# First two token tiles centred instead of normalised for their V products, and the last product of the kernel split over two banks and two store queues

## The chip, the cores and the metric

The kernel runs on one core of a Trainium2 chip. The metric is the device time of one execution in microseconds (us); the profile shows a "span" that is about 1.7 us shorter than that time, because it begins and ends with the recorded instructions. In some rounds the runs of the untouched kernel lay within 0.5 us of each other, in others they spread over as much as 2.3 us, so effects of one microsecond in 720 (0.14%) are at the edge of what can be timed. All runs quoted here are of the fast state; the lowest granted TensorE clock in any of them was 0.997 of full speed.

## The reference, cut to what matters

```python
def _layernorm(x, axis=-1, eps=1e-5):
    m = jnp.mean(x, axis=axis, keepdims=True)
    v = jnp.var(x, axis=axis, keepdims=True)
    return (x - m) / jnp.sqrt(v + eps)

# A_x: 1 x 2048 x 1024, A_wqkv: 1024 x 3072, all bf16
def _A_ref(x, wqkv, wo):                      # linear attention, 32 heads
    q, k, v = ...x @ wqkv...
    phi = lambda t: jnp.where(t > 0, t + 1, jnp.exp(t)) + 1e-6
    pq, pk = phi(q), phi(k)
    kv = jnp.einsum("bhsd,bhse->bhde", pk, v) # sum over all tokens
    z = jnp.einsum("bhsd->bhd", pk)
    # ... num / den, then @ wo

h = x + _A_ref(_layernorm(x), A_wqkv, A_wo)
h2 = h + _B_ref(_layernorm(h), ...)           # gated MLP, 1024 -> 3584 -> 1024
```

The change rests on one identity: a row of `_layernorm(x) @ Wv` is `rstd * ((x - m) @ Wv)`, where `rstd` is one number per token. So the product can start when the mean is known, and the scale can be applied when the result is copied out of PSUM.

## The kernel before: the parts that matter

There are 16 tiles of 128 tokens. For each, VectorE computes statistics and normalises; the normalised tile is transposed, on TensorE (`T1`) for tiles 0 to 3 and by a DMA transpose (`T1d`) for the later ones. Tiles 4 to 15 can then be multiplied in pairs with a Strassen scheme of seven products instead of eight (`sgroup`), which needs sums of weights and sums of x from VectorE. V of tiles 0 to 3 is done directly (`v_piece`), while weights and later tiles are still arriving. Tiles 5 and 6 take their statistics from ScalarE (`ln1_stats_act`: a pass for the mean, and one for the squares).

```python
def fin():                                    # last step of the VectorE statistics
    # bn_aggr (mean, variance), then variance + eps on VectorE, then power -0.5 on POOL
    ...

def v_piece(st, h, mid=None):                 # V of one tile, one half of the columns
    b = alloc_bank(P1_POOL)
    nt = ND2 + h
    for dc in range(NDC):
        if mid is not None and dc == NDC // 2:
            mid()
        mm(bank(b, NW), xnT[:, dc, st * P:(st + 1) * P], wkv[:, dc, nt * NW:(nt + 1) * NW], ...)
    v_copy(b, st, h)                          # ScalarE copies PSUM to SBUF

# sgroup, one Strassen group; X = tiles, W = weights, SX/TW = their sums; [...] cuts
prod(a, X(0, 0), W(0, 0), True, "P1")
ident_act(bank(b), bank(a), ..., name + "fk1")        # ScalarE copies a bank: the "fork"
hook(1)
prod(f, SX(2), TW(2), True, "P7")
# ...
prod(b, SX(1), TW(1), False, "P6")                    # P6 adds onto the fork
# fk2, hook(3), P2 and its phi, hook(4), P5, copy sc, hook(5), P4, hook(6), P3
# phi: ScalarE takes exp, VectorE does min/add and add/max; two of the four phis need
# a VectorE add first (add_phi). What is left over runs inside the NEXT group (pend).

# head
load_x1(0, split=True); load_x1(1); load_wkv(2, half=0, eng="act")
load_x1(2); load_wkv(2, half=1); load_x1(3); load_wkv(3)
pe_dummies(12, P1_POOL + [KVB])               # keep TensorE busy, to end its cold clock
# ... statistics, norm 0, load_wkv(1), T1(0), 3 dummies, norm 1, loads x 4, x 5, load_wkv(0)
v_piece(0, 0, lambda: T1(1))
v_piece(1, 0, lambda: T1(2))
# ... interleaved with weight sums twv/twk, x sums, norms 3 to 5 (see the diff)
k_group(0); v_group(2)                        # K of tiles 0 and 1; V of tiles 4 and 5
```

In the tail, the last product of the MLP accumulates two blocks of 256 columns in one PSUM bank; VectorE adds 512 columns at once and two stores go out on the queue of one engine (SyncE):

```python
for m in range(NM):
    for u in range(2):
        mm(ps[:, bk, u * HNW:(u + 1) * HNW], ...)
# ...
if last and (blk, dh) == (0, 1):
    dma(sl_fin[j], dst, src, "st_%d_%d" % (st, dh), reads=[bsrc])
```

Of the kernel before, what the change touches and what calls it, by code (L numbers as in the profile page):

```python
# [132 lines left out]
def bass_sequential_preLN__linear_attn_block__glu_gated_reglu__prompt_kernel(  # L133
# [71 lines left out]
    with es:  # L205
# [37 lines left out]

        RC = sb("RC", [P, NDC * D], bf16)
        TWk = RC[:].bitcast(f16).rearrange("p (j k c) -> p j k c", j=4, k=KH)
        Ssum = RC[:].bitcast(f16).rearrange("p (s k t) -> p s k t", s=4, k=KH)

# [148 lines left out]
        B_x1 = [bufs("x1_%d_" % i, NBC) for i in range(NX1)]  # L396
        B_xn = bufs("xn_", NXN)
        B_xnT = [bufs("xnT%d_" % s_, 2) for s_ in range(NST)]
        B_wkv = [bufs("wkv%d_" % i, 2) for i in range(NKV)]
# [4 lines left out]
        B_Sx = [bufs("Sx%d_" % i, NST // 2) for i in range(4)]  # L404
        B_at = _Buf("at")
        B_bt = bufs("bt_", 2)
        B_wo = bufs("wo_", ND2)
# [59 lines left out]
        def flat(x):  # L467
            return [b for row in x for b in (flat(row) if isinstance(row, list) else [row])]

        for i in range(2):  # L470
            for b_ in B_pk[NPK + i]:
                b_.over = B_x1[i]
# [299 lines left out]
        def ln_stats_steps(src_full, src_chunk_bufs, name):  # L772
            k = stat_ctr[0] % NSTAT
            stat_ctr[0] += 1

            def bn(c):
                PL.add("dve", lambda e: e.bn_stats(out=st6[:, k, c * 6:(c + 1) * 6],  # L777
                                                   in_=src_full[:, c * BCH:(c + 1) * BCH]),
                       reads=[src_chunk_bufs[c]], writes=[B_st6[k][c]], name=name + "_bn")

            def fin():
                PL.add("dve", lambda e: e.bn_aggr(out=mv[:, k, :], in_=st6[:, k, :]),
                       reads=B_st6[k], writes=[B_mv[k]], name=name + "_aggr")
                PL.add("dve", lambda e: e.tensor_scalar(out=rstd[:, k, :], in0=mv[:, k, 1:2], scalar1=EPS,
                                                        scalar2=None, op0=ALU.add),
                       reads=[B_mv[k]], writes=[B_rstd[k]], name=name + "_ve")
                PL.add("pool", lambda e: e.tensor_tensor(out=rstd[:, k, :], in0=rstd[:, k, :], in1=neghalf[:],
                                                         op=ALU.pow),
                       reads=[B_neghalf], writes=[B_rstd[k]], name=name + "_rstd")
            return k, [lambda: bn(0), lambda: bn(1), fin]  # L790

# [105 lines left out]
        def T1(st):  # L897
# [11 lines left out]
            partial.add(b)  # L909

        def T1d(st):
            k = st % NXN
# [12 lines left out]

        def v_piece(st, h, mid=None):
            b = alloc_bank(P1_POOL)
            nt = ND2 + h
            for dc in range(NDC):
                if mid is not None and dc == NDC // 2:  # L930
                    mid()
                mm(bank(b, NW), xnT[:, dc, st * P:(st + 1) * P], wkv[:, dc, nt * NW:(nt + 1) * NW],
                   dc == 0, dc == NDC - 1, [xnT_buf(st, dc), B_wkv[nt][0 if dc < WKH else 1]], B_bank[b],
                   "v_%d_%d" % (st, h))
            v_copy(b, st, h)

        def v_out(st, j):
# [6 lines left out]
        def v_copy(b, st, j):  # L944
            PL.add("act", lambda e: e.activation(out=v_out(st, j), in_=gw(bank(b)), func=ACTF.Identity),
                   reads=[B_bank[b]], writes=[B_v[st % NV][j]], name="v_%d_%d" % (st, j))

# [673 lines left out]
        def down_pass(ps_, fill):  # L1621
# [20 lines left out]
            def st_out(blk, dh, j, sl, src, bsrc):  # L1642
                st = ps_ * TPP + blk * STB + j
                dst = ov[st * P:(st + 1) * P, dh * NW:(dh + 1) * NW]
                if last and (blk, dh) == (0, 1):
                    dma(sl_fin[j], dst, src, "st_%d_%d" % (st, dh), reads=[bsrc])
                else:
# [27 lines left out]
            def q_add(dst, src, T, H, b, name):  # L1675
                d, bd = quad(dst, T, H)
                x, bx = quad(src, T, H)
                tt(d, qb(b), x, [B_bank[b]] + ([] if src is dst else bx), bd, name)

# [87 lines left out]

            def level2(pi, bks, Q, sg, evac):
                a, f, b, c = bks

                def prod(mi, bk, x, start):
# [5 lines left out]
                    if WSRC[pi][0] == "t" or WLIST[L][2][0] == "s":  # L1777
                        w = w.bitcast(f16)
                    for m in range(NM):
                        for u in range(2):  # L1780
                            mm(ps[:, bk, u * HNW:(u + 1) * HNW], xa[:, m, u * P:(u + 1) * P],
                               w[:, m * HNW:(m + 1) * HNW], start and m == 0 and u == 0, m == NM - 1,
                               xb + [B_wd[ws]], B_bank[bk], "d%d_%d_M%d" % (pi, ps_, mi), skip=True)
                    load_wd_next()
# [12 lines left out]
                def m6():  # L1797
                    prod(6, b, sg(1), False)
                    fork(c, b)

# [4 lines left out]
                def m5():  # L1805
                    prod(5, c, sg(0), False)
                    evac(5, c)

# [4 lines left out]
                def m3():  # L1813
                    prod(3, c, sg(3), False)
                    evac(3, c)

# [12 lines left out]
            level2(5, YB, q_11, sgs[5], ev_out(1, 0, V, O2, sl_out2))  # L1829
            level2(6, XB, q_d4, sgs[6], ev_out(0, 1, U, OS, sl_out))  # L1830

# [57 lines left out]
        load_wkv(2, half=0, eng="act")  # L1889
        act_warm()  # L1890
        load_x1(2)
        load_wkv(2, half=1)
        load_x1(3)
        load_wkv(3)

        pe_dummies(12, P1_POOL + [KVB])
        s0, s1_, s2_, s3 = [ln1_steps(st) for st in range(4)]
        for f_ in s0 + s1_[:1]:
            f_()
        ln1_norm(0)  # L1900
        load_wkv(1)
        T1(0)
        pe_dummies(3, [alloc_bank(P1_POOL)])
        for f_ in s1_[1:] + s2_[:1]:
            f_()
        ln1_norm(1)
        load_x1(4)
        load_x1(5)
        load_wkv(0)
        for f_ in s2_[1:] + s3[:1]:  # L1910
            f_()
        ln1_norm(2)
        for f_ in s3[1:]:
            f_()
# [3 lines left out]

        v_piece(0, 0, lambda: T1(1))
        v_piece(1, 0, lambda: T1(2))  # L1920
        ln1_norm(3)
        x_sums(0)
        v_piece(2, 0)
        m5, q5 = ln1_stats_act(5)
        m5()
        twv.pop(0)()
        v_piece(0, 1, lambda: T1(3))
        twk.pop(0)()
        ln1_stats(4)
        q5()  # L1930
        v_piece(1, 1)
        twk.pop(0)()
        ln1_norm(4)
        T1d(4)
        m6, q6 = ln1_stats_act(6)
        v_piece(3, 0)
        m6()
        ln1_norm(5)
        T1d(5)
        twk.pop(0)()  # L1940
        v_piece(2, 1)
        q6()
        twv.pop(0)()
        twk.pop(0)()
        twv.pop(0)()
# [54 lines left out]
        for p in range(NP_):  # L2000
            nq = NQ.get(p, (0, 0))
            hooks, sq = kv_hooks(p, nq)
            if p == NP_ - 1:
                hooks[7] = lambda: kvaccs(NP_ - 2)
# [236 lines left out]
```

## Time and profile before

The time before was 722.88 us (722.54 to 722.95, three runs). The page of the profiled run says where it goes. The first fence is from that page: span, busy table, busy tenths by fortieth of the span, and the chain that ended last.

```profile
span 721.0 us, 12872 instructions
PE 714.9 (99%) x4905; PEld 380.3 (53%) x4905; DVE 588.1 (82%) x1024; ACT 358.2 (50%) x623; POOL 110.7 (15%) x177
PE   8999999999999999999999999999999999999998
...
PE ps L763 94%; DMA RE<-RE 1%; DMA RAB<-RXH 1%; DVE RWG L981 0%; DMA RE<-in_A_x_dram 0%; ACT RXH L801 0%; PE ps L902 0%; DVE RX L1065 0%; DVE RE L1639 0%; DVE st L777 0%; DVE RXH L1230 0%; DVE RE L1126 0%; ACT RXH L1256 0%; DVE RW L956 0%; DVE RX L846 0%
```

TensorE (PE) is the bound, at 99% busy. Only its first and last fortieth show an 8. So only two places look worth anything: the microseconds before TensorE starts, and the tail. The Trainium skill ("TensorE: Matmul & The Clock Gate", Part 1: The HAM clock gate) says that a 512-column matmul starts every 426.7 ns while TensorE is cold and every 215.7 ns when warm. The trace agrees: 0.427 us for the dummies, 0.216 us later.

The timeline of TensorE in the first 34 us: start, duration of the group, engine, line, what it does, and in brackets how long TensorE sat idle before it and what ended the wait.

```profile
6.46 0.61 PE L902 MATMUL ps<-ident,RXH 128*128 128x128 bf16 x8 [0.50 <-DVE RXH L831]
...
7.85 1.02 PE L763 MATMUL ps<-RAB 128*128 128x512 bf16 x4
...
24.02 2.03 PE L763 MATMUL ps<-RC,RWG 128*128 128x512 f16 x8
25.89 1.03 PE L763 MATMUL ps<-RAB 128*128 128x512 bf16 x4
...
30.20 2.06 PE L763 MATMUL ps<-RW,RWG 128*128 128x512 f16 x8
```

The first V matmul starts at 7.85 us.

The timeline of VectorE (DVE), same kernel: the path to the first normalised tile, and then the last weight sums, the first phi of the K group (L846) and the first add of the K group (L1065).

```profile
4.93 0.15 DVE L784 TENSOR_SCALAR rstd<-mv 128x1 f32<-128x1 f32 x1
...
5.77 0.55 DVE L831 TENSOR_SCALAR RXH<-RE,mv,rstd 128x1024 bf16<-128x1024 bf16 x1
...
25.58 1.22 DVE L956 TENSOR_TENSOR RW<-RAB,RW 128x2048 f16<-128x2048 bf16 x1
27.58 0.29 DVE L846 TENSOR_SCALAR RX<-RX 128x512 bf16<-128x512 bf16 x1 [0.78 <-ACT RX L842]
...
28.84 0.68 DVE L1065 TENSOR_TENSOR RX<-ps,RX 128x512 f32<-128x512 f32 x1
```

Between 4.93 and 5.77 us the first tile waits for the variance and its power; this is what the change goes around.

The tail before, from the timeline of all engines:

```profile
714.83 2.67 PE L763 MATMUL ps<-RE,RAB 128*128 128x256 f16 x23
...
716.80 2.27 SPq L561 DMA_DIRECT2D out_dram<-RX  x4
717.54 0.69 DVE L1639 TENSOR_TENSOR RX<-ps,RE 128x512 bf16<-128x512 f32 x1 [0.77 <-PE ps L763]
```

The last matmul starts at 717.234; the last add takes 0.69 us; the last two stores are issued at 718.26 and 718.64 and land at 719.95 and 720.44.

### The profile page before, as it was taken

Reading aid. Unit: us, or ns where it says so; the run is one execution under the profiler, and the core shown is the slowest. Engines: PE = TensorE matmul, PEld = TensorE weight load, DVE = VectorE, ACT = ScalarE, POOL = GpSimd, SP = SyncE. Lnnn points to the kernel's source line nnn. Section 1 sums busy time; section 2 is a strip of 40 time slices with the busy share of each in tenths; the row PEclk is TensorE's granted clock in tenths of the full one; section 3 lists DMA queues with packets and bytes.
Section 4 is the critical chain, followed back from the end, with each engine's and each line's share of the span. In section 5 each row is a group of like instructions: output and inputs, shape, how many; then the busy total and the mean of one; then the engine's idle time right before and its main releaser. Section 6 shows DMA issues by size and latency. Waiting matters only on the chain.

```text
span 721.0 us, 12872 instructions
## 1 busy us (share of the span) xinstructions
PE 714.9 (99%) x4905; PEld 380.3 (53%) x4905; DVE 588.1 (82%) x1024; ACT 358.2 (50%) x623; POOL 110.7 (15%) x177
## 2 busy tenths in 40 slices
PE   8999999999999999999999999999999999999998
PEld 3444444444444444444444558865554555548887
DVE  7888867899776889888988787887889877887984
ACT  4877667764832466677756111144454545423010
POOL 2411100000450103331321001310000000000331
PEclk9999999999999999999999999999999999999999
DMA  9663244024998797999999999993464572037996
GB/s 313 212 106 72 46 132 160 3 30 76 217 229 257 223 287 232 275 303 316 301 271 271 305 257 324 314 216 114 140 179 128 161 256 72 1 103 252 323 316 177
DMA packets 192989, 143.64 MB, mean 199 GB/s; under 512 B 51872, under 2 KB 170400, under 8 KB 192928
## 3 DMA queue, kind: packets, MB, share of 16 engines
q1 hardware_dynamic: 188224, 138.50, 65.7%
q0 software_dynamic: 4032, 3.67, 3.5%
q8 instruction: 38, 0.62, 0.4%
q10 hardware_dynamic: 672, 0.66, 0.3%
q14 instruction: 23, 0.19, 0.1%
HBM read 98.76 MB, written 32.51 MB: 182 GB/s over the span
## 4 chain that ended last, share of the span: by engine, by line
PE 94%; DVE 2%; DMA 2%; issue 1%; ACT 1%; POOL 0%; SPq 0%; DVEq 0%; ACTq 0%
PE ps L763 94%; DMA RE<-RE 1%; DMA RAB<-RXH 1%; DVE RWG L981 0%; DMA RE<-in_A_x_dram 0%; ACT RXH L801 0%; PE ps L902 0%; DVE RX L1065 0%; DVE RE L1639 0%; DVE st L777 0%; DVE RXH L1230 0%; DVE RE L1126 0%; ACT RXH L1256 0%; DVE RW L956 0%; DVE RX L846 0%
## 5 line engine op out<-in xcount | busy, mean ns | idle before, releaser
L768 ACT ACTIVATE ps<-ps 128x512 f32<-128x512 f32 (+1 forms) x192 | 108.9, 567 | 221.5 <-PE ps L763 214.7
L763 PE MATMUL ps<-RC,RO 128*128 128x512 f16 x616 | 143.0, 369 | 0.0
L763 PE MATMUL ps<-RH,RWG 128*128 128x512 bf16 x448 | 108.1, 379 | 0.0
L763 PEld LDWEIGHTS ps<-RC,RO 128*128 128x128 f16 x616 | 60.3, 98 | 63.5
L763 PE MATMUL ps<-RC,RWG 128*128 128x512 f16 x320 | 76.8, 379 | 0.0
L763 PEld LDWEIGHTS ps<-RH,RWG 128*128 128x128 bf16 x448 | 43.8, 98 | 46.9
L1448 DVE TENSOR_TENSOR RAB<-ps,RAB 128x512 bf16<-128x512 f32 x56 | 37.3, 686 | 30.4 <-PE ps L763 30.4
L763 PE MATMUL ps<-RH,RO 128*128 128x512 bf16 (+1 forms) x256 | 61.2, 379 | 0.0
L1648 POOL DMA_DIRECT2D out_dram<-RX x20 | 17.9, 1256 | 263.3 <-DVE RX L1639 221.0
L763 PE MATMUL ps<-RW,RE 128*128 128x512 bf16 x256 | 57.6, 379 | 0.2 <-DMA RE<-RE 0.2
L763 PE MATMUL ps<-RAB 128*128 128x512 bf16 (+2 forms) x270 | 57.1, 351 | 0.1
L763 PE MATMUL ps<-RW,RAB 128*128 128x256 f16 (+3 forms) x362 | 52.9, 301 | 0.0
L763 PEld LDWEIGHTS ps<-RC,RWG 128*128 128x128 bf16 (+1 forms) x320 | 30.0, 98 | 39.8 <-ACT ps L768 5.8
L768 ACT ACTIVATE RE<-ps 128x512 f32<-128x512 f32 (+1 forms) x64 | 31.5, 503 | 37.8 <-PE ps L763 37.8
L763 PEld LDWEIGHTS ps<-RW,RAB 128*128 128x128 f16 (+1 forms) x362 | 35.3, 98 | 14.5
L1639 DVE TENSOR_TENSOR RE<-ps,RE 128x512 f32<-128x512 f32 x44 | 30.2, 687 | 14.3 <-PE ps L763 13.8
L768 ACT ACTIVATE RAB<-ps 128x512 bf16<-128x512 f32 x56 | 33.3, 594 | 16.9 <-PE ps L763 16.5
L1332 DVE TENSOR_TENSOR RO<-RWG 128x1024 f16<-128x1024 bf16 x54 | 36.9, 684 | 4.8 <-DMA RWG<-in_B_W_up_dram 4.8
L763 PEld LDWEIGHTS ps<-RH,RO 128*128 128x128 f16 (+1 forms) x256 | 24.4, 98 | 29.9 <-ACT RX L768 1.5
L1443 ACT ACTIVATE RAB<-RAB 128x1024 bf16<-128x1024 bf16 x28 | 29.5, 1055 | 19.2 <-DVE RAB L1434 18.6
L1434 DVE TENSOR_TENSOR RAB<-ps,RE 128x512 bf16<-128x512 f32 x56 | 37.2, 685 | 2.2 <-PE ps L763 1.9
L763 PEld LDWEIGHTS ps<-RAB 128*128 128x128 bf16 (+1 forms) x270 | 26.0, 98 | 24.4 <-ACT RAB L905 1.1
(163 smaller groups left out, 1159.1 us busy)
## 6 DMA issues: line engine op xcount, KB each, us to landing
RWG<-in_B_W_gate_dram SPq DMA_DIRECT2D x28, 512.0 KB, 6.2
RWG<-in_B_W_up_dram SPq DMA_DIRECT2D x28, 512.0 KB, 5.2
RW<-l_scr SPq DMA_DIRECT2D x20, 448.0 KB, 5.9
RW<-in_B_W_down_dram SPq DMA_DIRECT2D x14, 512.0 KB, 5.3
t_scr<-RW SPq DMA_DIRECT2D x14, 512.0 KB, 4.8
l_scr<-RX SPq DMA_DIRECT2D x7, 1024.0 KB, 6.0
RE<-l_scr SPq DMA_DIRECT2D x15, 448.0 KB, 5.6
RE<-in_A_x_dram SPq DMA_DIRECT2D x23, 256.0 KB, 3.7
```

What stands on the lines that cost most here:

```text
L763: lambda e: e.matmul(out_ap, lhsT, rhs, start=start, stop=stop, skip_group_check=skip),
L768: PL.add("act", lambda e: e.activation(out=dst, in_=src, func=func), reads=reads, writes=writes, name=name)
L1332: PL.add(eng, lambda e: e.tensor_tensor(out=tb(j, u), in0=f0(u), in1=f1(u), op=ALU.subtract), reads=[B_w[i + x] for x in r] + ([B_T[k + x] ...
L1434: PL.add("dve", lambda e: e.tensor_tensor(out=d, in0=src, in1=ftmp[:, u, :], op=ALU.add), reads=[bsrc, B_s5[u]], writes=[db], name=name)
L1443: PL.add("act", lambda e: e.activation(out=d, in_=d, func=ACTF.Relu), reads=[], writes=db, name=name)
L1448: PL.add("dve", lambda e: e.tensor_tensor(out=d, in0=bank(b), in1=d, op=ALU.mult), reads=[B_bank[b]], writes=[db], name=name)
L1639: PL.add(eng, lambda e: e.tensor_tensor(out=dst, in0=in0, in1=in1, op=op), reads=reads, writes=writes, name=name)
L1648: PL.add("pool", lambda e: e.dma_start(dst, src, accum_op=ALU.add), reads=[bsrc], writes=[B_hscr[st]], slot=sl, name="acc_%d_%d" % (st, dh))
```

## The change

The intent is twofold. In the head, tiles 0 and 1 are centred in halves as soon as their mean is known, transposed on TensorE, and multiplied; the copy of their V products from PSUM applies `rstd`. Their normalised versions are still needed for K and Q, so they are made too, and are now transposed by two DMA transposes. In the tail, the two halves of the last product go to two PSUM banks, one half first; VectorE adds the first half while TensorE computes the second, and the stores alternate between the queues of SyncE and ScalarE.

The core of the diff (cuts marked with `...`):

```diff
+        def centre(st, hf):
+            PL.add("dve", lambda e: e.tensor_scalar(out=xn[:, 2 + st, c], in0=x1[:, st, c], scalar1=mv[:, k, 0:1],
+                                                    scalar2=None, op0=ALU.subtract), ...)
+        def T1c(st, hf):
+            ... # four 128x128 transposes of the centred half on TensorE, one ScalarE copy to xcT
         def v_copy(b, st, j):
-            PL.add("act", lambda e: e.activation(out=v_out(st, j), in_=gw(bank(b)), func=ACTF.Identity),
+            sc, rd = (1.0, []) if st >= 2 else (rstd[:, v_k[st], :], [B_rstd[v_k[st]]])
+            PL.add("act", lambda e: e.activation(out=v_out(st, j), in_=gw(bank(b)), func=ACTF.Identity, scale=sc),
...
         act_warm()
-        load_x1(2)
         load_wkv(2, half=1)
-        load_x1(3)
+        load_x1(2)
         load_wkv(3)
+        load_x1(3)
-        pe_dummies(12, P1_POOL + [KVB])
+        pe_dummies(9, [KVB] + P1_POOL)
...
+        for hf in range(2):
+            centre(0, hf)
+            T1c(0, hf)
+        pe_dummies(2, [alloc_bank(P1_POOL)])
... # the same for tile 1; load_wkv(1) in between
         ln1_norm(0)
-        T1(0)
+        T1d(0)                                # DMA transpose, then load of x tile 4
...
         ln1_norm(1)
-        load_x1(4)
-        load_x1(5)
+        T1d(1)                                # DMA transpose, then load of x tile 5
         load_wkv(0)
...
-        v_piece(0, 0, lambda: T1(1))
-        v_piece(1, 0, lambda: T1(2))
+        v_piece(0, 0, {5: lambda: T1c(1, 0), 7: lambda: T1c(1, 1)})
+        ln1_norm(2)
+        v_piece(1, 0)
... # V pieces, weight sums, x sums and statistics in a new order
-        m6, q6 = ln1_stats_act(6)
+        m6, q6a, q6b = ln1_stats_act(6, True) # squares of tile 6 in two halves, inside the K group
         v_piece(3, 0)
         m6()                                  # mean of tile 6: still in front of the K group
...
+            if p == 0:
+                hooks[1], hooks[3] = q6a, q6b
```

```diff
 # tail
-                    dma(sl_fin[j], dst, src, "st_%d_%d" % (st, dh), reads=[bsrc])
+                    dma(sl_fin[j], dst, src, "st_%d_%d" % (st, dh), reads=[bsrc], eng=("sp", "act")[j % 2])
...
-                    for m in range(NM):
-                        for u in range(2):
-                            mm(ps[:, bk, u * HNW:(u + 1) * HNW], ...)
+                    two = isinstance(bk, tuple)
+                    for m, u in [(m, u) for u in range(2) for m in range(NM)] if two else \
+                            [(m, u) for m in range(NM) for u in range(2)]:
+                        bu = bk[u] if two else bk
+                        mm(ps[:, bu, u * HNW:(u + 1) * HNW], ...)
```

## The prediction

> **What bounds the kernel.** TensorE. The page gives PE 99% busy of a 721.0 us span; the busy table by stage shows PE full in nearly every stretch after 60 us, and the wait list for PE between 26 and 700 us has only 0.5 us. A warm 512-column matmul starts every 0.216 us, a 128-column transpose every 0.056 us. So only two places are worth anything: the time before TensorE runs gaplessly, and the tail after its last matmul.
>
> **Head, before (timeline).** Tile 0 lands at 3.34-3.51 us; statistics 3.36-4.89; variance add 4.93; power on POOL 5.17-5.74; normalise 5.77-6.32; transposes 6.46; ScalarE copy 7.11; first V matmul 7.85. TensorE then runs to the first K product at about 23.15 us with one 0.14 us gap.
>
> **Head, after.** Centring needs only the mean; half a tile is about 0.3 us (0.55 us for 1024 columns). So transposes start near 5.35, the copy of the first half near 5.8, the first V matmul near 6.5: 1.35 us earlier, with as many transposes and matmuls as before. The nine cold dummies (0.427 us each) still cover the cold clock, which ended at 5.16 us. Scaling on the four V copies reads a per-partition operand; the Trainium skill ("ScalarE: Activation LUTs", What ACT_TABLE_LOAD costs) puts about 93 ns on each; no run has shown it here, and it is off the path.
>
> **What takes some back.**
> - Loads are serial: 256 KB per 0.68 us, 512 KB per 1.5 us by their landings. The second half of the first V weights should land near 7.4 us (needed 7.4), x tile 2 near 8.1 instead of 6.64, so the third tile's normalise ends near 11.6: TensorE waits about 0.3 us.
> - VectorE, second busiest up to 52 us, gets four centrings (+1.2 us).
> - Two DMA transposes (about 1.1 us of all DMA engines each) now sit among the loads. The first K weights land near 20 us (17.7 before; needed 22.2), x tile 6 near 22 us. Its mean on ScalarE stands in front of the copy that opens product 6 of the first K group: TensorE may wait about 0.6 us there.
> - VectorE's chain to the first KV accumulation (34.9 us, where TensorE already waited 0.33 us) comes only about 0.6-0.9 us earlier.
>
> Net head gain: 0.8 us (0.2 to 1.3).
>
> **Tail.** Before: last matmul ends near 717.5; one 128x512 add of 0.69 us to 718.23; stores issued at 718.26 and 718.64 on one queue, landed 719.95 and 720.44. After: the first half is summed under the second half's seven matmuls (7 x 0.109 us), 128x256 takes about 0.42 us, the last store is issued at once on the other queue: about 0.7 us saved. Two banks are needed because two engines must not touch one bank at once (Trainium skill, "PSUM — Partial Sum Buffer", PSUM bank collisions). Two 128x256 forks for one of 128x512 cost ScalarE 0.15 us, hidden.
>
> **Sum.** 722.88 - 0.8 - 0.7, rounded: 721.3 us, a gain of 0.2%. 80% range 720.1 to 722.6. Faster by over 2%: 0.01; within 2%: 0.98; slower by over 2%: 0.01.
>
> **What would show it.** First V matmul near 6.5 us; first K product near 22.2 (23.15 before); first KV accumulation 0.6-0.9 us earlier than 34.9; from there a constant lead to the last matmul; last store landing 2.3 us after the last matmul instead of 2.9.
>
> **What would make it wrong.** DMA transposes that hold up the loads by several us (the first K group waits for weights, the head gain vanishes); or the ScalarE mean and VectorE backlog costing nothing (then near 720.7).

## More of the kernel before

The eight matmuls at 24.02 are P7 and P6 of the first K group, the eight at 30.20 are P7 and P6 of the next group (V of tiles 4 and 5). In both, P6 follows P7 almost without a break (0.13 and 0.16 us from the start times of the single matmuls).

Note the 0.78 us: VectorE's list of sums ends at 26.80, and it then waits for ScalarE. That is all the slack VectorE has at this point.

ScalarE (ACT), same kernel: the mean of x tile 6 and, behind it in ScalarE's order, the fork that P6 of the K group needs.

```profile
21.31 1.06 ACT L801 ACTIVATE RXH<-RE 128x1024 bf16<-128x1024 bf16 x1 [0.42 <-DMA RE<-in_A_x_dram]
...
24.36 0.60 ACT L768 ACTIVATE ps<-ps 128x512 f32<-128x512 f32 x1
```

## The result, and the profile after

The changed kernel took 723.08 us (median of four runs, 722.52 to 723.54) against 722.85 us for the kernel before in the same rounds (722.54 to 722.95, four runs). The ratio is 1.0004, with a 95% interval of 0.9986 to 1.0021. Ratios here are the mean time of one kernel's fast runs over that of the other's of the same rounds, so they are not quite the ratio of the medians quoted. The predicted gain of 1.6 us, a ratio of 0.9978, lies outside that interval: it did not come. The time of 723.08 lies outside the predicted range of 720.1 to 722.6.

The lines of the page that answer to those of before, now for the kernel after:

```profile
span 721.8 us, 12822 instructions
PE 710.7 (98%) x4846; PEld 380.0 (53%) x4901; DVE 589.0 (82%) x1030; ACT 358.9 (50%) x626; POOL 111.4 (15%) x178
...
PE ps L769 93%; DMA RE<-in_A_x_dram 2%; SPq L567 1%; ACT RXH L809 0%; DVE RWG L1016 0%; DVE RE L857 0%; DVE RX L1100 0%; ACT ps L774 0%; DVE RE L1674 0%; DVE RX L854 0%; DVE st L783 0%; DVE RW L991 0%; SPq L571 0%; ACT RX L850 0%; DVE RWG L1614 0%
```

The span is 0.8 us longer. The chain has a new second entry: 2% of the span, some 14 us, now runs through loads of x (`in_A_x_dram`), and the queue of SyncE (`SPq`) with its DMA transpose (L571) is on it. Before, the loads of x were at 0%.

TensorE, kernel after, the same stretch as before:

```profile
6.67 1.02 PE L769 MATMUL ps<-RAB,RC 128*128 128x512 bf16 x4
7.90 0.39 PE L769 MATMUL ps<-RAB,RC 128*128 128x512 bf16 x1 [0.21 <-DMA RAB<-in_A_wqkv_dram]
...
23.23 1.03 PE L769 MATMUL ps<-RC,RWG 128*128 128x512 f16 x4
25.67 1.04 PE L769 MATMUL ps<-RC,RWG 128*128 128x512 f16 x4 [1.42 <-ACT ps L774]
...
30.86 1.03 PE L769 MATMUL ps<-RW,RWG 128*128 128x512 f16 x4
32.12 1.04 PE L769 MATMUL ps<-RW,RWG 128*128 128x512 f16 x4 [0.23 <-ACT ps L774]
```

The first V matmul is 1.18 us earlier, as intended, and P7 of the first K group is still 0.79 us ahead of before. Then P6 of the K group waits for the fork on ScalarE. Counted from one matmul start to the next, less the usual 0.216 us, that wait is 1.58 us, and 0.39 us at P6 of the following group, where before had 0.13 and 0.16. So the lead of 0.79 us becomes a lag of 0.90 us (-0.79 + 1.45 + 0.24).

ScalarE, kernel after, says what the fork was waiting behind:

```profile
23.50 1.06 ACT L809 ACTIVATE RXH<-RE 128x1024 bf16<-128x1024 bf16 x1 [1.12 <-DMA RE<-in_A_x_dram]
...
25.03 0.59 ACT L774 ACTIVATE ps<-ps 128x512 f32<-128x512 f32 x1
```

The mean of x tile 6 started at 23.50 (before: 21.31), when the tile had landed. The fork stood behind it.

VectorE, kernel after: the new centrings, the last weight sum, the first phi and the first add.

```profile
5.01 0.62 DVE L922 TENSOR_SCALAR RXH<-RE,mv 128x512 bf16<-128x512 bf16 x2
...
26.70 1.23 DVE L991 TENSOR_TENSOR RW<-RAB,RW 128x2048 f16<-128x2048 bf16 x1
28.47 0.29 DVE L854 TENSOR_SCALAR RX<-RX 128x512 bf16<-128x512 bf16 x1 [0.55 <-ACT RX L850]
...
29.74 0.68 DVE L1100 TENSOR_TENSOR RX<-ps,RX 128x512 f32<-128x512 f32 x1
```

The last weight sum ended 1.13 us later than before (27.93 against 26.80), and the first phi and the first add came 0.9 us later. The first matmul that accumulates KV followed at 35.80 instead of 34.91.

The tail after:

```profile
715.80 3.22 PE L769 MATMUL ps<-RE,RAB 128*128 128x256 f16 x28
...
718.32 0.81 SPq L567 DMA_DIRECT2D out_dram<-RX  x2
718.33 1.54 ACTq L567 DMA_DIRECT2D out_dram<-RX  x2
719.06 0.42 DVE L1674 TENSOR_TENSOR RX<-ps,RE 128x256 bf16<-128x256 f32 x1 [0.34 <-PE ps L769]
```

The last matmul starts at 718.751 and the last store, issued at 719.52, lands at 721.215: 2.46 us from one to the other, against 3.21 us before (720.44 - 717.234). The tail gave 0.75 us. Its parts can be read off: the last add is 0.27 us shorter (0.42 instead of 0.69), the last store is issued 0.04 us after that add instead of 0.41 (it no longer follows another store on the same queue), and it lands 1.70 us after its issue instead of 1.80. No run had only one of the two edits, the two banks or the two queues.

The landing times, read from the semaphore records of the DMA engines, are these. "first" and "last" are the first and the last of the 16 DMA engines; the transfer is complete at the last.

| load | before, issued | first / last | after, issued | first / last |
|---|---|---|---|---|
| first V weights, half 0 | 1.23 | 5.61 / 5.82 | 1.24 | 5.87 / 6.36 |
| first V weights, half 1 | 2.18 | 7.78 / 8.12 | 1.72 | 7.36 / 7.86 |
| DMA transpose of tile 0 | none | | 8.32 | 16.01 / 16.17 |
| x tile 4 | 7.09 | 15.16 / 15.49 | 12.55 | 16.74 / 16.79 |
| DMA transpose of tile 1 | none | | 13.09 | 17.51 / 17.70 |
| x tile 5 | 9.20 | 15.84 / 16.18 | 15.18 | 18.29 / 18.99 |
| second half of the first K weights | 10.10 | 18.85 / 19.19 | 16.27 | 21.12 / 22.77 |
| x tile 6 | 11.41 | 19.51 / 21.23 | 16.89 | 21.81 / 23.41 |

Two things show. Everything behind the transposes is 1.3 to 3.6 us late at its last landing. And the last landing of x tile 6 trails the first by 1.6 to 1.7 us in both kernels. The Trainium skill ("DMA: Bandwidth & Descriptors", Why a DMA increments its semaphore by 16 and not by 1) says that the engines of one transfer finish independently and only the full count means that all data is there; the trace agrees. In both traces one engine had a packet of instruction fetch (16 KB; 1.10 us from 18.96 before, 0.93 us from 19.34 after) among its work shortly before; whether that made it the late one, the trace does not say.

### The profile page after: what moved, and what is told of

The parts are those of the page before. It is cut to its first block, busy times and chain, and to the rows that moved or that the text cites. A ratio compares the mean times of both kernels' runs of the same rounds, so it can differ in the third digit from the quotient of the medians.

```text
span 721.8 us, 12822 instructions
## 1 busy us (share of the span) xinstructions
PE 710.7 (98%) x4846; PEld 380.0 (53%) x4901; DVE 589.0 (82%) x1030; ACT 358.9 (50%) x626; POOL 111.4 (15%) x178
## 4 chain that ended last, share of the span: by engine, by line
PE 93%; DMA 2%; DVE 2%; issue 1%; ACT 1%; SPq 1%; ACTq 0%
PE ps L769 93%; DMA RE<-in_A_x_dram 2%; SPq L567 1%; ACT RXH L809 0%; DVE RWG L1016 0%; DVE RE L857 0%; DVE RX L1100 0%; ACT ps L774 0%; DVE RE L1674 0%; DVE RX L854 0%; DVE st L783 0%; DVE RW L991 0%; SPq L571 0%; ACT RX L850 0%; DVE RWG L1614 0%
## 5 line engine op out<-in xcount | busy, mean ns | idle before, releaser
L769 PE MATMUL ps<-RH,RO 128*128 128x512 bf16 (+1 forms) x228 | 55.2, 379 | 1.5
L769 PE MATMUL ps<-RAB 128*128 128x512 bf16 (+2 forms) x237 | 49.7, 348 | 0.1
L769 PEld LDWEIGHTS ps<-RW,RE 128*128 128x128 bf16 x256 | 24.0, 98 | 28.7 <-DVE dtmp L1236 0.6
```

What stands on the lines that cost most here:

```text
L769: lambda e: e.matmul(out_ap, lhsT, rhs, start=start, stop=stop, skip_group_check=skip),
```

## The experiments

Fifteen kernels ran, one of them twice (`e4` and `e4b`). Each edit is given against the kernel before or after. The texts in quotes use letters for theories; the sense is the one that the text gives. The theories are these:

- **Late load.** The two DMA transposes delay x tile 6; its mean on ScalarE holds the fork; TensorE waits at P6 of the K group.
- **VectorE's list.** The four centrings (two took 0.62 us, so 1.2 us in all) and their later waits lengthen VectorE's list; whatever lead TensorE has, it waits for VectorE (directly or through ScalarE) at the next group.
- **Both, one behind the other.** Taking the first away only uncovers the second.
- **Rivals.** The order of ScalarE's own work; the DMA transposes as such, by their place in the queue; the tail not paying.

All results (us; "before" is the kernel before of the same rounds):

| run | base and edit | median (range), runs | before | ratio (95%) |
|---|---|---|---|---|
| e1_tail | before + tail | 722.11 (721.83-722.44), 5 | 722.79 | 0.9987 (0.9975-0.9999) |
| e2_head | before + head | 724.14 (723.62-725.05), 5 | 722.79 | 1.0017 (1.0005-1.0030) |
| e3_x6_first | after, x tile 6 loaded before K weights | 723.06 (722.97-726.53), 6 | 722.79 | 1.0010 (0.9994-1.0025) |
| e4_mean_later | after, mean of tile 6 behind the fork | 723.24 (722.04-724.28), 5 | 722.79 | 1.0001 (0.9989-1.0013) |
| e4b_mean_later | the same again | 722.26 (722.05-722.58), 4 | 722.69 | 0.9994 (0.9981-1.0008) |
| e6_pe_transposes | after, TensorE instead of DMA transposes | 724.22 (723.72-724.85), 5 | 722.53 | 1.0022 (1.0010-1.0034) |
| e7_transposes_last | after, the transposes last in the queue | 723.14 (722.71-723.72), 5 | 722.53 | 1.0007 (0.9994-1.0019) |
| e8_last_and_mean | e7 and e4 | 723.36 (723.04-723.79), 5 | 722.53 | 1.0010 (0.9998-1.0022) |
| e9_before_two_transposes | before + two idle DMA transposes | 725.51 (724.13-727.75), 6 | 722.53 | 1.0042 (1.0028-1.0057) |
| e10_norm_on_act | after, norms 0 and 1 on ScalarE | 723.16 (722.57-723.27), 5 | 722.69 | 1.0004 (0.9991-1.0018) |
| e11_norm_act_mean | e10 and e4 | 722.34 (722.09-722.67), 5 | 722.69 | 0.9995 (0.9983-1.0008) |
| e12_before_centrings | before + four idle centrings | 723.79 (722.99-724.57), 5 | 722.69 | 1.0014 (1.0001-1.0026) |
| e13_mean_and_pool | e4, one weight sum on POOL | 722.87 (722.79-723.52), 5 | 723.60 | 0.9993 (0.9980-1.0005) |
| e14_norm_mean_pool | e11, one weight sum on POOL | 722.41 (722.07-722.69), 5 | 723.60 | 0.9985 (0.9971-0.9998) |
| e15_one_sum_less | e4, one weight sum left out (wrong result) | 721.87 (721.40-724.04), 5 | 722.47 | 0.9988 (0.9975-1.0002) |
| e16_squares_later | e4, squares of tile 6 later too | 722.03 (721.99-722.74), 5 | 722.47 | 0.9992 (0.9980-1.0005) |

No ratio is clear of 1 by more than half a per cent, and many intervals hold 1. So most of the argument below rests on the profiled runs, where one can follow the lead or lag of TensorE against the kernel before from mark to mark. "Lead" means the start of the same instruction on TensorE, compared with the profiled run of before. A profiled run is a single execution.

### Head and tail apart

`e1_tail` is the kernel before with only the tail part of the diff; `e2_head` is the kernel before with only the head part.

```diff
 # e1_tail: of the change, only these
+                if isinstance(b, tuple): ...            # two adds of 256 columns
+            c2 = (c, spare) if spare is not None else c
+    level2(6, XB, q_d4, sgs[6], ev_out(0, 1, U, OS, sl_out), YB[3] if last else None)
+    ... eng=("sp", "act")[j % 2]
 # e2_head: everything else
```

> The kernel before with only the tail of the change (last product's halves in two banks, its stores on two queues). Theory A (the tail gained about 0.75 us, as the profile of after shows: 2.46 us from the last matmul's start to the last landing instead of 3.21, and the head gave it back): 0.6 to 0.8 us under before. Rival T (the tail gained nothing in the timed runs): same as before within 0.2 us.

> The kernel before with only the head of the change (centred tiles, scale on the copy, new order of loads). Theory A: the head loses what the tail gains: 0.5 to 1.3 us over before, with the 1.6 us wait of TensorE before product 6 of the first K group. Rival T (head and tail both near zero): within 0.2 us of before.

The tail alone is 0.9987 and the head alone 1.0017; the product is 1.0004, which is the ratio of the whole change. In us, the tail gives 0.9 and the head costs 1.2 (by the medians 0.7 and 1.35), where 0.7 and a gain of 0.8 were predicted; both intervals only just exclude 1. In the trace of `e1_tail` TensorE runs as before up to its last matmul (it starts at 717.154, before 717.234), and the span is 720.2 instead of 721.0. In that of `e2_head` the wait at P6 of the K group is there again, at 1.85 us, TensorE lags by 0.97 us at 32 us, and by 0.84 us at the end. So the tail did what it should, and the fault lies in the head.

### Is it the late load of x tile 6?

`e3_x6_first` puts the load of x tile 6 ahead of the first K weights, and `e4_mean_later` takes the mean of tile 6 from in front of the fork.

```diff
 # e3_x6_first, against after
-        load_wkv(0)
...
         ln1_norm(2)
+        load_wkv(0)
 # e4_mean_later and e4b_mean_later, against after
         v_piece(3, 0)
-        m6()
...
-                hooks[1], hooks[3] = q6a, q6b
+                k4_ = hooks[4]
+                hooks[1], hooks[3], hooks[4] = m6, q6a, lambda: (q6b(), k4_())
```

> After with the load of x tile 6 put before the two loads of the first K weights. Theory A (the mean of tile 6 on ScalarE waits for tile 6, and the copy that opens product 6 stands behind it): tile 6 lands near 20 instead of 23.4 us, TensorE's wait there falls from 1.58 to about 0.6 us (the mean itself, 1.25 us, still stands before the copy), total about 0.9 us under after. Rival B (VectorE's backlog after four more centrings is the limit): the total stays within 0.3 us of after, the wait moves to the second V group or the first KV accumulation.

> After with the mean of tile 6 moved on ScalarE behind the copy that opens product 6 of the first K group, its squares two products later; loads as in after. Theory A: that wait of 1.58 us is gone, perhaps 0.2 us at product 5; total 1.1 to 1.5 us under after. Rival B (VectorE): as for the run before, at most 0.3 us.

> The kernel with the mean of tile 6 moved, again, because the profile of its first run fell on an execution in which one DMA engine brought the first weights 2.3 us late. Theory AB: where the first weights land near 6.2 us, no wait before product 6 of the first K group, but product 6 of the second V group still starts no earlier than 31.8 us, because VectorE's first K result comes near 28 us. Theory A2 alone: product 6 of the second V group starts near 30.6 us.

The profiled runs of `e3` and of the first `e4` were spoilt by something else: one of the 16 DMA engines delivered the first V weights late (last landing 8.49 and 8.18 us instead of 6.36), so TensorE stood still for 1.8 and 2.1 us between 6 and 9 us. In `e4` it then ran its matmuls at 0.427 us until 11.7 us, that is, with the cold clock. For that reason `e4` was run again as `e4b`. Its profiled run was clean: the lead of 1.07 us at P7 is still 1.07 behind P6. The wait of 1.58 us at P6 is down to 0.16. So the late load is a cause of that wait, and the order of ScalarE's work is how it reached TensorE. But the lead did not last. TensorE, VectorE and ScalarE of `e4b`:

```profile
31.35 1.04 PE L769 MATMUL ps<-RW,RWG 128*128 128x512 f16 x4 [0.58 <-ACT ps L774]
```

```profile
20.99 1.23 DVE L991 TENSOR_TENSOR RC<-RAB 128x2048 f16<-128x2048 bf16 x1 [0.76 <-DMA RAB<-in_A_wqkv_dram]
...
27.71 0.29 DVE L854 TENSOR_SCALAR RX<-RX 128x512 bf16<-128x512 bf16 x1
```

```profile
29.69 0.63 ACT L850 ACTIVATE RX<-RX 128x512 bf16<-128x512 f32 x1 [0.70 <-DVE RX L1100]
```

VectorE's first phi starts at 27.71 with no wait just before it: VectorE has become the limit. (Before, it came at 27.58 after a wait of 0.78.) But earlier in its list, at 20.99, VectorE had waited 0.76 us for K weights, which stand behind the transposes; so its lateness here is not all work of its own. ScalarE idles 0.70 us for VectorE's add (L1100), and the fork of the next group stands behind that exp. P6 of the next group waits 0.74 us, P3 of the K group had waited 0.47, and the lead of 1.07 us is a lag of 0.13 at 32 us and of 0.02 at the end. The span, 720.3 us, is that of the tail alone (720.2). `e3`'s timed runs do not differ from after's (five of its six are between 722.97 and 724.01), and its profile says nothing clean. `e4b` fell between its two forecasts: P6 of the next group started at 31.35, earlier than the 31.8 of theory AB and later than the 30.6 of A2.

### Is it the DMA transposes?

`e6` makes the transposes of tiles 0 and 1 on TensorE again; `e7` puts the two DMA transposes behind all the early loads; `e8` is `e7` with the mean moved. `e9` goes the other way: it adds two DMA transposes, into a space that nobody reads, to the kernel before.

```diff
 # e6_pe_transposes, against after
-        T1d(0)
+        load_x1(4)
-        T1d(1)
+        load_x1(5)
-        v_piece(1, 1)
-        v_piece(2, 0)
+        v_piece(1, 1, {4: lambda: T1(0)})
+        v_piece(2, 0, {4: lambda: T1(1)})
 # e7_transposes_last, against after: loads as in e6, then
         ln1_norm(2)
+        for st in range(2):
+            dma_t(sl_tx[st], xnT[:, :, st * P:(st + 1) * P], xn[:, st, :], "T1d_late", ...)
... # x_sums(0) moves behind two of the K weight sums; scratch of tile 5's mean moves
 # e8_last_and_mean: e7, and m6 moved as in e4
 # e9_before_two_transposes, against before
-        load_x1(4)
-        load_x1(5)
+        for st in range(2):
+            dma_t(sl_tx[st], xcT[:, st], xn[:, st, :], "extra", ...)
+            load_x1(4 + st)
```

> After with the two early DMA transposes done on TensorE instead (16 transposes of 0.056 us, 0.9 us of TensorE). Theory A2 (the two transposes sit in the one queue of loads and make every load behind them about 2.2 us later, and TensorE, 0.8 us ahead, now meets those loads; which wait ends last, weights or tile 6, changes with the order): x tile 6 lands again near 21.2 us, K weights near 17.7 and 19.2, the 1.6 us wait before product 6 of the first K group falls under 0.3 us; total 0.3 to 0.7 us under after. Rival B (four centrings on VectorE): total 0.9 us over after (the price of the transposes).

> After with the two DMA transposes behind the K weights and x tile 6 in the queue, and VectorE's sums of tiles 0 and 1 behind the two K weight sums that need only weights. Theory A2: wait before product 6 falls from 1.6 to about 0.6 us, total about 0.9 us under after. Rival B: within 0.3 us of after.

> The same and the mean of tile 6 moved behind the copy that opens product 6. Theory A2: no wait over 0.3 us in the first K group, total 1.2 to 1.5 us under after, the fastest so far. Rival B: within 0.3 us of after.

> The kernel before with two DMA transposes more, into a place nothing reads, at the same place among the loads where the change has them; nothing else. Theory A2: loads behind them 2.2 us later, x tile 6 near 23.4 us, TensorE waits 1.0 to 1.6 us in the first K group, total 0.9 to 1.5 us over before. Rival B: no change.

`e9` is the clearest. Two transposes that compute nothing cost the kernel before 3 us (1.0042). TensorE's timeline shows where:

```profile
21.21 6.22 PE L766 MATMUL ps<-RAB 128*128 128x512 bf16 x27 [3.09 <-ACT RAB L908]
```

x tile 5 landed at 19.45 instead of 16.18, ScalarE's mean of tile 5 waited for it, and the copy of transposed tile 3 stood behind that mean. The lag is 3.1 us at 32 us and 2.8 us at the end. SyncE's issue of the first transpose occupied its queue for 5.07 us here and 4.11 us in the kernel after, that of the second for 2.07 and 2.04 us, and later loads on that queue were issued only afterwards. This is not the price of a transpose alone. From 22 to 40 us the same traces have transposes of the same shape whose issue took 1.2 to 1.3 us (one in `e9` took 2.06), and in the kernel before two plain loads at 4.9 and 7.1 us took 2.06 and 2.01 us to issue, where most took 0.4 to 0.5. The long issues fall where many loads are outstanding; that this backlog makes them long was not tested. The 3 us are also twice what was expected of `e9` (0.9 to 1.5), since the late load met another place of ScalarE's order than the one named. That the transposes delay the loads is therefore shown, and that such a delay reaches TensorE through ScalarE's order too.

But removing the delay is not enough. In `e6` x tile 6 landed at 19.92 and P6 of the K group waited only 0.36 us. With the 16 transposes back on TensorE (16 times 0.056 us) its lead at P7 was only 0.05 us, and VectorE's first add came 0.42 us late, so that the lag at 32 us was 0.41 us. Two further waits of 1.2 and 1.3 us, at 167 and 239 us, made it 2.7 us at the end; the trace puts both to VectorE, but nothing here says why it was late. In `e7` and `e8` the lag just behind P6 of the K group was nothing (-0.08 and -0.02 us), but VectorE now waited for the late transposes (in `e7` 1.32 us before norm 4 and 0.31 us before x sum 0), and its first phi came at 29.16 and 29.22 us. P6 of the next group then waited 1.36 and 1.29 us, for a lag of 1.6 us in both. Both were forecast to gain 0.9 to 1.5 us over after if only the loads mattered; neither did. Wherever the transposes go, the time is lost at the next place.

### Is it VectorE's list?

`e12` adds the four centrings, and nothing else, to the kernel before, just in front of x sum 0. `e10` and `e11` take work off VectorE: the norms of tiles 0 and 1 are made on ScalarE from the centred copies (with `e11` also moving the mean).

```diff
 # e12_before_centrings, against before
         ln1_norm(3)
+        for i in range(4):
+            PL.add("dve", lambda e, i=i: e.tensor_scalar(..., scalar1=mv[:, 2, 0:1],
+                                                         scalar2=None, op0=ALU.subtract), ...)
         x_sums(0)
 # e10_norm_on_act, against after
-        ln1_norm(0)
-        T1d(0)
-        ln1_norm(1)
-        T1d(1)
-        load_wkv(0)
+        def norm_act(st): ...      # activation, Identity, scale=rstd, from xn[2 + st] to xn[st]
+        v_piece(0, 0, {5: ..., 7: lambda: (T1c(1, 1), norm_act(0), norm_act(1))})
+        T1d(0)
+        T1d(1)
+        load_wkv(0)
 # e11_norm_act_mean: e10, and m6 moved as in e4
```

> The kernel before with four centrings more (about 1.2 us of VectorE) into a place nothing reads, before the first sums of tiles 0 and 1; loads and TensorE as before. Theory AB: VectorE has little idle time up to 52 us, so TensorE waits 0.5 to 1.0 us more in the second V group or the first KV accumulation; total 0.4 to 1.0 us over before. Theory A2 alone: same as before within 0.2 us.

> After with the full normalisation of tiles 0 and 1 (two operations of 0.55 us on VectorE, needed only for the DMA transposes) done on ScalarE from the centred copies; loads in the same order. Theory A2 alone (only loads are late): same as after within 0.3 us. Theory AB (the loads and VectorE's backlog hold TensorE at about the same time, so that removing one leaves the other): VectorE's chain up to the first K result about 0.5 to 1 us earlier where it does not wait, but the 1.6 us wait before product 6 stays: total 0 to 0.4 us under after.

> The same and the mean of tile 6 moved behind the copy that opens product 6 (both suspected waits relieved). Theory AB: first K result on VectorE near 27.5 us (28.47 in after), product 6 of the second V group starts near 31.2 us (32.12 in after), total 0.7 to 1.2 us under after, near 722.0. Theory A2 alone: as the mean moved alone (0 to 0.3 us under after).

`e12` costs 1.0014, or 1.0 us, with an interval that just excludes 1. In its profiled run the first phi came at 28.01 instead of 27.58, and now without a wait. VectorE (the four centrings and the phi) and TensorE (P6 of the next group) of `e12`:

```profile
13.21 1.14 DVE L1925 TENSOR_SCALAR RC<-RXH,mv 128x512 bf16<-128x512 bf16 x4
...
28.01 0.28 DVE L848 TENSOR_SCALAR RX<-RX 128x512 bf16<-128x512 bf16 x1
```

```profile
31.64 1.04 PE L765 MATMUL ps<-RW,RWG 128*128 128x512 f16 x4 [0.17 <-ACT ps L770]
```

So the added work used up the slack of 0.78 us, and the phi came 0.43 us late; the lag of TensorE at 32 us was 0.42 us, and 0.31 at the end. Not all of this is the centrings: they hold VectorE for 1.05 us (13.21 to 14.26), and this execution was already 0.24 us late in front of them (norm 3 at 12.75 instead of 12.51) and 0.10 us late at P7 of the K group. About 0.3 us of TensorE's lag (0.42 less 0.10) is theirs. The timed 1.0 us is more, but its interval begins at 0.1 us, and one of the five times (724.57) is 3.2 us over its span instead of the usual 1.7. By the spans the medians differ by 0.5 us (721.4 against 720.9).

`e10` and `e11` freed about 1.0 us on VectorE, but VectorE then waited 0.94 and 1.09 us for the first K weights, which had landed at 21.5 and 21.3 us. The weights stand behind the DMA transposes, so the freed time could not be used. In `e11`, then, VectorE was late through a wait for weights more than through work. `e10` waited 1.94 us at P6 of the K group; `e11`, with the mean moved, led by 0.74 there, lagged by 0.45 at 32 us and by 0.06 at the end. Timed, `e11` was 0.7 us under after, at the low edge of what theory AB expected.

### Can VectorE be relieved so that it counts?

`e13` and `e14` move one V weight sum from VectorE to POOL, in four pieces. `e15` leaves the sum out altogether and puts zeros in its place. Its result is wrong (relative error 0.83), but its timing is that of a kernel whose VectorE has one 1.2 us sum less. `e16` tests the rival that it is the order of ScalarE's work: the two halves of the squares of tile 6 move later.

```diff
 # e13_mean_and_pool: e4, and
+        twv.pop(1)
+        def twv_pool(kk):
+            PL.add("pool", lambda e: e.tensor_tensor(out=tw_v(0)[:, kk, :], ..., op=ALU.subtract), ...)
... # four calls behind v_piece(1, 0)
 # e14_norm_mean_pool: e11, and the same
 # e15_one_sum_less: e4, and
+        PL.add("pool", lambda e: e.memset(TWv[:, 0], 0.0), writes=[B_TWv[0]], name="twv0")
+        twv.pop(1)
 # e16_squares_later: e4, but
+                hooks[1] = m6
+                hooks[4], hooks[5] = lambda: (q6a(), k4_()), lambda: (q6b(), k5_())
```

> The kernel with the mean of tile 6 moved, and one of VectorE's weight sums (1.22 us, the first of the V sums) given to POOL in four pieces. Theory AB (VectorE's backlog takes back the 1.07 us of lead that TensorE had at product 6 of the first K group): VectorE's first K result about 0.5 us earlier (27.2 instead of 27.71), the wait of 0.74 us before product 6 of the second V group halves, total 0.3 to 0.7 us under the mean moved alone, near 721.7. Rival C (ScalarE, with the moved mean in the first K group, takes it back): VectorE finishes earlier and then waits for ScalarE, TensorE as before, total within 0.2 us of the mean moved alone (722.3).

> The same with the full normalisation of tiles 0 and 1 on ScalarE too. Theory AB: VectorE waits for the K weights near 21 us instead, so little on top: within 0.3 us of the run before. Rival C: ScalarE has more to do, 0 to 0.4 us slower than the run before.

> The kernel with the mean of tile 6 moved, and one of VectorE's weight sums (1.22 us) left out altogether: POOL fills its place with zeros before VectorE starts, so the result is wrong on purpose and POOL takes no time beside VectorE. Theory AB (VectorE's backlog): the wait of 0.74 us before product 6 of the second V group falls under 0.4 us and TensorE keeps more of its lead; total 0.3 to 0.8 us under the mean moved alone (722.26), near 721.7. Rival C (ScalarE's order): VectorE finishes 1.2 us earlier and waits for ScalarE; total within 0.2 us of 722.26.

> The kernel with the mean of tile 6 moved, and its two squares on ScalarE one and two products later still, with nothing taken off VectorE. Rival C: the 0.47 us wait before product 3 of the first K group goes, total 0.3 to 0.5 us under 722.26. Theory AB: that wait goes too, but the time turns up before product 6 of the second V group, where VectorE is as late as before; total within 0.2 us of 722.26.

POOL was no relief. VectorE of `e13`, the K weight sum that ran beside POOL's pieces:

```profile
17.56 2.17 DVE L991 TENSOR_TENSOR RC<-RAB 128x2048 f16<-128x2048 bf16 x1
```

The same sum takes 1.22 us elsewhere, and a norm beside POOL took 1.29 us instead of 0.55. The Trainium skill ("SBUF — State Buffer", Who interferes with whom) says that a VectorE instruction with two SBUF inputs contends with a GpSimd (POOL) instruction that reads SBUF, that a `tensor_scalar` such as the norm can contend too, in a two-port mode, and that the one of the two that issues later is held up. The trace agrees that they hold each other up: what VectorE lost on three instructions (0.95, 0.74 and 0.75 us) is more than the 1.2 us it was spared. `e14`'s ratio of 0.9985 leans on a high set of runs of before (median 723.60); its own median of 722.41 is no better than `e4b`'s 722.26. So `e13` missed the gain that theory AB forecast, and because of POOL the two runs say little about that theory.

`e16` took away the wait before P3 of the K group, and its lead there was 0.79 us. Then P6 of the next group waited longer, 1.07 instead of 0.74 us. TensorE and VectorE of `e16`:

```profile
31.34 1.04 PE L769 MATMUL ps<-RW,RWG 128*128 128x512 f16 x4 [0.90 <-ACT ps L774]
```

```profile
28.96 0.68 DVE L1100 TENSOR_TENSOR RX<-ps,RX 128x512 f32<-128x512 f32 x1
```

VectorE's first add, which before was at 28.84, is at 28.96: 0.12 us late. TensorE's lag behind P6 is 0.12 us. `e4b` had 28.97 and a lag of 0.13. The two kernels reach P6 with different leads, and leave it together, at the time VectorE sets. This speaks against the order of ScalarE's work in the K group as the cause of what is left. Timed, `e16` was 0.23 us under `e4b`, between the two forecasts, so the trace has to decide.

The traces of all runs can be asked the same question. In sixteen of the eighteen profiled runs, before and after among them, P6 of that group starts 2.37 to 2.38 us after VectorE's first add (before: 31.22 and 28.84; after: 32.12 and 29.74), however early TensorE was. The other two are `e4` and `e15`, where the first weights were so late that TensorE did not wait there (2.45 us). So VectorE's add sets this place, in the kernel before too. Why the add is late differs. In after, VectorE still waited 0.55 us for ScalarE in front of the first phi, so there the late fork set it: without that wait the phi would have come about 0.26 us after that of before (an estimate, from 26.70 and the 1.14 us between the same two starts in `e4b`), and not 0.9. In `e4b`, `e7`, `e8` and `e11` VectorE had waited for transfers, and in `e16` 0.45 us for the statistics of tile 5, which came at 23.7 us instead of 21.7. Only `e12` has the centrings alone. How the lateness of `e4b` and `e16` divides between the centrings and these waits was not separated.

`e15` was meant as the counter-proof. Its profiled run had the late DMA engine again (8.09 us), so its offset to before is of no use, but the waits are. VectorE and TensorE of `e15`:

```profile
29.79 0.29 DVE L855 TENSOR_SCALAR RX<-RX 128x512 bf16<-128x512 bf16 x1 [1.46 <-ACT RX L851]
```

```profile
32.65 1.89 PE L770 MATMUL ps<-RW,RWG 128*128 128x512 f16 x8
```

With one sum less, VectorE has 1.46 us of slack at the first phi, and P7 and P6 of the next group run through as eight matmuls without a break. Its four other runs took 721.40 to 722.58 us, and the lowest three are below every run of `e4b` and `e16`. The median is 0.4 us below `e4b`'s; this fits, but is too small to be called a measured gain. The late run also shifts VectorE and TensorE against each other, since the loads were not as late as TensorE was, so this profile alone is not a clean proof; that VectorE's add sets the time of P6 rests on the agreement of the sixteen runs above, and what the centrings cost on `e12`.

### The late DMA engine at the start

In four of the fourteen profiled runs that contain the new head (`e3`, `e4`, `e13`, `e15`) the last engine delivered the first V weights at 7.5 to 8.5 us, in the other ten at 5.9 to 6.4. The four profiled runs with the old head had 5.8 to 6.1. The old head uses the weights at 7.85 us, so lateness up to about 2 us would cost it next to nothing. The new head uses them at 6.67 us and pays. In two of those four runs the wait (2.0 and 2.1 us) also brought the cold clock back. This fits with the wider spread of many kernels with the new head, but how often it happens in runs without a profile was not seen, and why the engine is late stays open.

## Why the prediction was wrong

- **The tail was right.** Predicted about 0.7 us; the traces gave 0.75, and the tail alone was timed at 0.9 us faster.
- **The start of the head was right.** The first V matmul was predicted near 6.5 and came at 6.67 us. "The second half of the first V weights should land near 7.4 us" was 7.86, which cost 0.37 us. The third tile's norm was predicted to end near 11.6 and ended at 11.9. The first K product was predicted near 22.2 and came at about 22.4. The scale on the copy is an operand read per partition, for which the skill ("ScalarE: Activation LUTs", What ACT_TABLE_LOAD costs) gives 93 ns: the copies took 0.69 us with it and 0.60 without, so 0.09 us, off the path.
- **Step that failed, first part: "x tile 6 near 22 us ... TensorE may wait about 0.6 us there."** It landed at 23.41 us and the wait was 1.58 us. The delay by the transposes, twice 1.1 us, was estimated well (23.41 - 21.23 = 2.18). What was wrong is the time it was added to, which must have been near 19.8 us: in the profile of before, x tile 6 began to be complete at 19.51 us, but its last DMA engine landed at 21.23 us. A load must be timed at its last engine.
- **Step that failed, second part: "VectorE's chain ... comes only about 0.6-0.9 us earlier."** The first KV accumulation came 0.9 us later. The prediction named the 1.2 us of centrings, but did not put them against VectorE's slack in that stretch, 0.78 us at the first phi. In after itself the late fork still came last: VectorE waited 0.55 us for ScalarE before the phi, and about 0.26 of the 0.9 us would have been left without it. Where the late load was taken out of TensorE's way (`e4b`, `e16`), VectorE did not wait in front of the phi, its add came 0.12 to 0.13 us later than before, and TensorE's lead of up to 1.07 us was gone at P6 of the next group. So "Net head gain: 0.8 us" was not to be had from this change: VectorE sets the time at which the head ends, and the change put work on VectorE and late transfers in front of it. How much of VectorE's lateness is the one and how much the other stays open; the centrings alone cost about 0.3 us (`e12`).
- **"From there a constant lead to the last matmul" was nearly right, with the sign turned.** The lag was 0.90 at 32 us, 0.68 at 45 us, 0.96 at 105 us, and in this run 1.47 from 198 us on. The last step, 0.5 us in the attention-output stage, appears in after's profiled run and not in `e2_head`'s (0.84 us at the end). The trace puts it to a wait for VectorE; why VectorE was late there was not traced.
- **Sum.** In the profiled runs, lag 1.52 us at the last matmul less 0.75 us of the tail gives 0.77 us, which is the difference of the spans (0.8). Timed, the median is 0.23 us above before.

The named failure mode, "DMA transposes that hold up the loads by several us ... the head gain vanishes", describes half of what happened. The other failure mode, "VectorE backlog costing nothing", pointed at the right engine with the wrong sign.

The best correct versions were `e16` (722.03 us), `e1_tail` (722.11) and `e4b` (722.26). All have the tail; the head adds nothing measurable to it in any of them. Keeping only the tail part is the simplest choice, and it is a gain of about 0.1%.

Open: the two late waits in `e6` at 167 and 239 us; the step at 198 us in after's profiled run; how VectorE's lateness divides between the centrings and its waits; and the late DMA engine.

## What to carry to other kernels

When the bound engine is started earlier, ask which engine sets the time at the next meeting point, and how much slack it has there: here VectorE had 0.78 us, and the change gave it 1.2 us more work, and put late transfers in front of some of it, so a lead of 1.1 us on TensorE was worth nothing. A transfer that replaces work of a busy engine takes a place in a serial queue, and everything behind it is late; time it by its last DMA engine, and look for in-order work on another engine (here a mean on ScalarE) that will wait for it in front of something urgent. Then cut the change in two and time the parts: here that showed at once that one half paid and the other cost.

## What the Trainium skill lacked or had wrong

- "DMA: Bandwidth & Descriptors", DMA Transpose (X-bar): it gives no time for which the issue of a DMA transpose holds the issuing queue (elsewhere the page has cycle counts of "previous generations" beside those of trn3 B0, and none for a queue with loads outstanding). Here the first held SyncE's queue for 4.11 us (5.07 in `e9`) and the second for 2.04 us (2.07), and the loads behind were issued only afterwards; most later ones between 22 and 40 us took 1.2 to 1.3 us.
- The same page, Latency and other measured facts, has 261 GB/s for one kind of DMA transpose and 350 to 400 for the contiguous case. Here a transpose of 256 KB landed 0.86 and 0.91 us after the transfer ahead of it (16.17 - 15.31 and 17.70 - 16.79), which is some 290 to 305 GB/s if they ran one behind the other (an estimate), between the two figures; a plain load of 256 KB took 0.69 us (16.18 - 15.49).
- The same page says that the 16 engines finish independently, but not by how much. Here the last trailed the first by up to 0.7 us in most rows of the table of landing times, by 1.6 to 1.7 us for x tile 6 and, in after, for the second half of the first K weights (an instruction-fetch packet of 0.9 to 1.1 us came shortly before), and by 1.6 to 3.0 us for the first V weights in four of the fourteen profiled runs with the new head.
- "TensorE: Matmul & The Clock Gate", Part 1: its table has the cold clock return after an idle window of about 3.4 us. Here waits of 1.99 us (`e15`) and 2.12 us (`e4`), soon after the first warm matmuls, were followed by matmuls at 0.427 us for 3.0 to 3.4 us; waits of 1.40 us (`e13`), 1.80 us (`e3`) and even 3.47 us (`e9`, up to 21.21 us) were not. So the length of the wait alone does not decide it.
- "SBUF — State Buffer", Who interferes with whom, was borne out (1.22 us grew to 2.17 us). "PSUM — Partial Sum Buffer", PSUM bank collisions, which the prediction cites, was not put to the test: no run let two engines touch one bank at once.
